# Threshold attention into a leaky MLP on one Trainium2 core: 128-partition loads with heads p and p+4 paired, MoE in groups of 128 tokens fed each step, weight loads gated by step

## Chip, core and metric

The kernel runs on one core of one Trainium2 (trn2) chip. The metric is device time in microseconds (us); lower is better. A "run" below is one timed execution. A run over 1.5% above the fastest of the same kernel in the same rounds counts as slow: one run of the kernel before (671.7 us) did and is left out of the ratios. A kernel has one profiled execution, so a stage read from a profile carries more noise than a time. Profiles of kernels that have the same program up to the 18th step show that step up to about 5 us apart. I therefore do not interpret stage differences under about 5 us.

The profile's engine names are PE (TensorE, matrix products), PEld (its weight loads), DVE (VectorE), ACT (ScalarE), POOL (GpSimd) and SP (SyncE, which issues most of the DMA transfers). L189 is a line of the kernel. A "chain of waits" is the work that ended last, followed back piece by piece to what released it.

## The reference

```python
# q, k, v: (8 batches, 8 heads, 576 rows, 64), float32; tau = 0.02
scores = q @ k^T / 8
scores = where(scores >= rowmax - tau, scores, -1e9)
attn   = softmax(scores);  x = (attn @ v), heads joined -> (4608 tokens, 512)
h = x @ w_in                     # w_in (512, 2048)
out = max(0.01*h, h) @ w_out     # w_out (2048, 512)
```

The kernel calls the second part the MoE, though it is one dense layer pair.

## The kernel before

Work proceeds in **steps**: one head pair times 128 query rows (the last 64 rows of two pairs share a step). There are 8 batches of 18 steps, 144 in all. A step does the scores (PE), a running max and shift (DVE), exp (ACT), a DMA transpose of the weights w into wt on SP's queue, and four steps later the product pv. In the profile's lines km and qm are the loaded k and q, sc the scores, sf and mx the scaled scores and their row maximum, P the shifted scores, xT the attention's result, hp and op the products of the hidden and output units below, gT the hidden values. k and q are split into high and low fp16 parts and transposed by DMA into kst and qst.

```python
def load_pair(src, store, nm, b, p):          # 64 partitions per load, heads 2p and 2p+1
    hb, g = divmod(p, 2)
    ...
    nc.sync.dma_start(out=store[b, hb][ds(64 * g, 64), :, :],
        in_=src[b, ds(2 * p, 2), :, :].rearrange("h (p t) d -> p h (t d)", t=9))
```

The MoE is cut into hidden units (h, 8 matmuls of 256 columns for a group of 256 tokens) and output units (o). The leak 0.01*h costs no vector work: `relu(0.99 h)` goes through w_out, and `x @ W_io`, with W_io = 0.01 * w_in @ w_out, is one more matmul in each output unit. W_io must be built first, from four DMA transposes of w_in (winT) and 64 matmuls (wiop).

```python
for g in range(4):                            # 1 MB each of float32, cast on the way
    at(1 + g // 2, lambda g=g: load_w_in(g))  # at(s, f): f is issued at the end of step s
    at(3 + g // 2, lambda g=g: load_w_out(g))
for g in range(2):
    at(6 + g, lambda g=g: wio_turn(g))
...
credit = min(credit + (1.1 if live else 2.0), 2.5)
if s >= 8 and wq:                             # W_io is built in steps 8 to 15
    hu = [wq.popleft(), wq.popleft()]
while credit >= 1.0 and (hq or oq):
    f = next_h(); ...
    f = next_o() if not wq and s >= 16 else None
```

Of the kernel before, what the change touches and what calls it, by code (L numbers as in the profile page):

```python
# [16 lines left out]
def kernel(  # L17
# [18 lines left out]

    nc = tc.nc
    B, H, S, D = q.shape
    tau_f = float(tau)
    NP = H // 2  # L40
# [3 lines left out]
    LAG = 4  # L44
    NJ = DF // 128
    NEG = -1025.0
    NW = 4

# [25 lines left out]
    def load_pair(src, store, nm, b, p):  # L74

        hb, g = divmod(p, 2)
        if (b, hb) not in store:
            store[b, hb] = sb.tile([128, 2, 576], FP32, tag=nm, bufs=2, name=nm)
        nc.sync.dma_start(  # L79
            out=store[b, hb][ds(64 * g, 64), :, :],  # L80
            in_=src[b, ds(2 * p, 2), :, :].rearrange("h (p t) d -> p h (t d)", t=9))

    def load_v(b, i):

        if i == 0:
            vts[b] = vbufs[b % 2]
        vt = vts[b]
        sv = v[b, :, :, :].rearrange("(g h) (p t) d -> h p g (t d)", h=2, t=9)
        out_, in_ = [
            (vt[0:64, :, 0, 0:5, :], sv[0][:, :, 0:320]),  # L90
            (vt[64:128, :, 0, 0:4, :], sv[0][:, :, 320:576]),
            (vt[64:128, :, 1, 0:5, :], sv[1][:, :, 0:320]),
            (vt[0:64, :, 1, 1:5, :], sv[1][:, :, 320:576]),
        ][i]
        nc.gpsimd.dma_start(out=out_, in_=in_)
# [53 lines left out]
    anchor = [None]  # L149

    def after_anchor(ins):

        if anchor[0] is not None:
            tc.add_manual_dep(
                ins.ins, anchor[0].ins.name,
                mybir.DependencyInfo(mybir.DependencyClass.Sync, mybir.DependencyReason.DATA), reason="port")


    class Group:
        def __init__(self, n, stores):  # L160
            self.n = n
            self.x = sb.tile([128, 4, n], FP16, tag=f"xT{n}", bufs=5 if n == 256 else 2, name="xT")
            self.g = None
            self.stores = stores
# [5 lines left out]
    def next_h():  # L170

        if hq and (hq[0][1] > 0 or live_g[0] < 2):
            f, u = hq.popleft()
            if u == 0:
                live_g[0] += 1
            return f
# [9 lines left out]
    late = []  # L186
    tail = [False]
# [3 lines left out]
    def h_unit(G, u):  # L191
        n = G.n
        per = 512 // n

        def mms():
            if u == 0:
                G.g = sb.tile([128, NJ, 256], FP16, tag="gT", bufs=2, name="gT")[:, :, 0:n]
            hp = ps.tile([128, per, n], FP32, tag="h", bufs=2, name="hp")
            for jj in range(per):
                j = u * per + jj  # L200
                for g in range(4):
                    mm(hp[:, jj, :], w_in16[:, g, ts(j, 128)], G.x[:, g, :], g == 0, g == 3)

            def act():
                nc.scalar.activation(out=G.g[:, ds(u * per, per), :], in_=hp, func=AF.Relu, bias=0.0, scale=0.99)  # L205
                if (u + 1) * per == NJ:
                    for m in range(n // 128):
                        for c in range(4):
                            oq.append((lambda m=m, c=c: o_unit(G, m, c), m == n // 128 - 1 and c == 3))
# [3 lines left out]
    def o_unit(G, m, c):  # L213
        if c == 0:
            if tail[0]:
                t = len(late) % 4
                late.append(0)
                G.op = ps.tile([128, 2, 512], FP32, tag=f"sc{t % 2}", bufs=1, name="op")[:, 0, :] if t < 3 else ps.tile([128, 512], FP32, tag="o", bufs=1, name="op")
            else:
                G.op = ps.tile([128, 512], FP32, tag="o", bufs=1, name="op")  # L220
        mm(G.op, G.x[:, c, ds(128 * m, 128)], w_io16[:, c, :], c == 0, False)
        for j in range(4 * c, 4 * c + 4):
            mm(G.op, G.g[:, j, ds(128 * m, 128)], w_out16[:, j, :], False, j == NJ - 1)
        if c == 3:
            op = G.op

            def fin():
# [5 lines left out]
                return lambda: nc.sync.dma_start(out=G.stores[m], in_=osb)  # L233
# [10 lines left out]
    def wio_unit(g, c):  # L244
        def mms():
            if c == 0:
                w_inT["ps", g] = ps.tile([128, 512], FP32, tag="o", bufs=1, name="wiop")
            p_ = w_inT["ps", g]
            for j in range(4 * c, 4 * c + 4):
                mm(p_, w_inT[g][:, j, :], w_out16[:, j, :], j == 0, j == NJ - 1)  # L250
            if c == 3:
                if g + 2 < 4:
                    wio_turn(g + 2)
                return lambda: nc.scalar.activation(out=w_io16[:, g, :], in_=p_, func=AF.Copy, bias=0.0, scale=0.01)
            return None
# [18 lines left out]
    def group_of(b, c):  # L274

        if c == 4:
            key = ("t", b // 4)
            if key not in groups:
                t = b // 4
                groups[key] = Group(256, [rows_of(4 * t + 2 * m, 4) for m in range(2)])  # L280
            return groups[key], 64 * (b % 4), b % 4 == 3
        if (b == B - 1 and c >= 2) or (b == 0 and c < 2):
            if (b, c) not in groups:
                groups[b, c] = Group(128, [rows_of(b, c)])
            return groups[b, c], 0, True
        key = (b, c // 2, 0)
        if key not in groups:
            groups[key] = Group(256, [rows_of(b, 2 * (c // 2) + cc) for cc in range(2)])
        return groups[key], 128 * (c % 2), c % 2 == 1
# [26 lines left out]
    def pv(s):  # L316
# [17 lines left out]
        def evac():  # L334


            if c < 4:
                x_ = G.x[:, :, ds(col, 128)].rearrange("f g (p i) -> f g i p", i=2)
# [3 lines left out]
            else:  # L342
                m, i = divmod(col // 64, 2)
                x_ = G.x[:, :, ds(128 * m, 128)].rearrange("f g (p i) -> f g i p", i=2)[:, :, i, :]
# [4 lines left out]
            if done:  # L349
                for u in range(NJ * G.n // 512):  # L350
# [35 lines left out]
    R = [ds(0, 64), ds(64, 64)]  # L386
    for p in range(NP):
        load_pair(k, kms, "km", 0, p)
        load_pair(q, qms, "qm", 0, p)
    def prep(p, nm, eng):  # L390
        hb, r = p // 2, R[p % 2]
        for h in range(2):
            if eng == "pool":
                x64(nm, 0, hb, h, r)
            for part in PARTS[nm]:
                lo(nm, 0, hb, h, part, r, eng)
        turn(nm, 0, p)

    for p in range(4):
        hb, r = p // 2, R[p % 2]  # L400
        hi("k", 0, hb, r)
        hi("q", 0, hb, r, "act" if p else "dve")
    for p, nm, eng in ((0, "q", "dve"), (0, "k", "dve"), (1, "k", "dve"), (1, "q", "dve"),
                       (2, "q", "dve"), (2, "k", "pool"), (3, "k", "pool")):
        prep(p, nm, eng)
    at(0, lambda: prep(3, "q", "dve"))

    for b in range(1, B):
        s0 = 18 * (b - 1)
        for hb in range(2):  # L410
            t0 = s0 + 9 * hb
            for i, p in enumerate((2 * hb, 2 * hb + 1)):
                at(t0 - 7 + 2 * i, lambda b=b, p=p: load_pair(k, kms, "km", b, p))
                at(t0 - 6 + 2 * i, lambda b=b, p=p: load_pair(q, qms, "qm", b, p))
# [17 lines left out]
    def load_w_in(g):  # L432
        nc.gpsimd.dma_start(out=w_in16[:, g, :], in_=moe_w_in[ts(g, 128), :])

    def load_w_out(g):
        nc.gpsimd.dma_start(
            out=w_out16[:, ds(4 * g, 4), :],
            in_=moe_w_out[ds(512 * g, 512), :].rearrange("(j p) d -> p j d", p=128))

    for i in range(4):  # L440
        at(0, lambda i=i: load_v(0, i))
    for g in range(4):
# [125 lines left out]
```

## Time and profile before

Before: 667.9 us median (663.6 to 672.0, 4 runs); the profiled span is 666.1 us. I cut the span where the 18th, the 36th and the last step start their shift (`P<-sf,mx` on DVE).

| stage | before, us |
|---|---|
| start: first batch, to the 18th step | 129.3 |
| second batch | 70.2 |
| later six batches | 417.2 |
| tail, after the last step's shift | 49.4 |

The view of busy time by stretch, for these stages of the kernel before. Columns are the stretch, its length, the busy us of each engine, the granted PE clock, the share of the 16 DMA engines (1.08 in the start: the packets' times there sum to more than the stretch, so they overlap) and GB/s.

```profile
core 0: us, PE busy (x) PEld busy (x) DVE busy (x) ACT busy (x) POOL busy (x), PEclk, DMA share, GB/s
0.00:129.30 129.30, 56.27 (x585) 32.92 (x587) 62.44 (x178) 57.40 (x116) 39.02 (x56) 0.97 1.08 169
129.30:199.50 70.20, 59.26 (x632) 34.97 (x633) 52.14 (x168) 52.79 (x115) 18.70 (x24) 0.93 1.04 182
199.50:616.70 417.20, 369.15 (x4007) 221.91 (x4007) 313.61 (x1003) 322.46 (x700) 92.67 (x121) 0.96 0.98 166
616.70:666.10 49.40, 43.74 (x367) 27.39 (x364) 5.70 (x13) 14.22 (x27) 0.00 (x0) 0.99 0.18 54
```

In the start PE works 56 of 129 us while the DMA share is 1.08, which points to DMA as the limit. In the later batches PE works 88% of the time. In the tail PE works 44 of 49 us.

The chain of waits of before, in order of time: start us, length, what the chain waited on.

```profile
32.35 15.42 DMA km<-in_k_dram
...
50.98 15.03 DMA wt<-w
66.31 15.14 DMA wt<-w
...
85.94 5.56 DMA winT<-win
91.54 3.48 PE wiop L189 x8
95.02 1.79 PE hp L189 x32
98.05 1.83 PE wiop L189 x8
102.02 1.83 PE wiop L189 x8
```

The line `hp x32` shows that 32 matmuls of 128 columns take 1.79 us, 56 ns each.

Groups of instructions of before with shapes kept apart (busy us, mean ns of one, then the idle time before them):

```profile
L189 PE MATMUL hp<-xT,win 128*128 128x256 f16 x1024 | 133.2, 277 | 0.0
L189 PE MATMUL hp<-xT,win 128*128 128x128 f16 x256 | 16.6, 219 | 0.0
L189 PE MATMUL wiop<-wout,winT 128*128 128x512 f16 x64 | 16.8, 410 | 7.1 <-DMA winT<-win 7.1
L339 DVE TENSOR_TENSOR xT<-pv,wt 128x512 f16<-128x512 f32 x32 | 23.3, 727 | 12.9 <-PE pv L327 12.9
```

Busy time divided by count gives 130 ns for a matmul of 256 columns and 65 ns for one of 128: no loss from halving the group. The mean ns of one (277 and 219) is longer because consecutive matmuls overlap in the trace.

### The profile page before, as it was taken

The numbers are of one execution on the slowest core, as the hardware profiler recorded it, in microseconds if no ns is written. First come the engines' busy times: TensorE is split into PE (matmuls) and PEld (weight loads), VectorE is DVE, ScalarE is ACT, GpSimd is POOL, SyncE is SP. The second block draws the span as 40 slices with busy tenths as digits, with TensorE's granted clock in tenths as the row PEclk, the third lists the DMA queues.
The fourth block names the chain that finished last, engine by engine and source line by source line (L and its number), as shares of the span: only waits on it lengthen the run. The fifth ranks groups of instructions, "written<-read, shape, count | busy, mean of one in ns | idle before, by whom it ended". The sixth has DMA issues, their size and how long they took to land.

```text
span 666.1 us, 14773 instructions
## 1 busy us (share of the span) xinstructions
PE 528.4 (79%) x5584; PEld 317.2 (48%) x5584; DVE 433.9 (65%) x1358; ACT 446.9 (67%) x955; POOL 150.4 (23%) x200
## 2 busy tenths in 40 slices
PE   0203359879796979699879989799979996999997
PEld 0101236546363646355445645465645563656564
DVE  5605337858786878578765858678756976888201
ACT  5115238759786888678785868689767886878421
POOL 3605112113331332024211422133202420000000
PEclk9999979989898989799998989999989998999999
DMA  9999999999999999979996999999998999557301
GB/s 183 136 154 166 182 186 159 189 168 165 186 206 153 164 177 194 178 151 181 198 180 123 191 180 184 162 167 191 202 165 173 178 170 148 105 107 124 85 32 47
DMA packets 298887, 106.35 MB, mean 160 GB/s; under 512 B 275264, under 2 KB 285504, under 8 KB 298816
## 3 DMA queue, kind: packets, MB, share of 16 engines
q1 hardware_dynamic: 287424, 96.50, 83.0%
q0 software_dynamic: 11392, 8.92, 10.9%
q8 instruction: 43, 0.70, 0.4%
q14 instruction: 28, 0.23, 0.1%
HBM read 36.70 MB, written 9.44 MB: 69 GB/s over the span
## 4 chain that ended last, share of the span: by engine, by line
PE 51%; DMA 22%; DVE 12%; ACT 9%; SPq 3%; issue 2%; POOL 0%; ACTq 0%
PE op L189 19%; PE hp L189 14%; DMA wt<-w 13%; PE sc L303 10%; DVE sf L363 8%; PE pv L327 5%; DMA qst<-qs 5%; ACT P L492 3%; DMA km<-in_k_dram 3%; ACT w L481 3%; PE wiop L189 2%; DVE P L477 2%; SPq L79 1%; ACT ks L125 1%; PE sc L309 1%
## 5 line engine op out<-in xcount | busy, mean ns | idle before, releaser
L363 DVE TENSOR_SCALAR_CACHE_REDUCE sf<-sc 128x576 f32<-128x576 f32 x288 | 206.5, 754 | 133.8 <-PE sc L303 122.8
L481 ACT ACTIVATE w<-P 128x576 f16<-128x576 f16 x288 | 193.6, 675 | 29.6 <-DVE P L477 16.9
L303 PE MATMUL sc<-kst,qst 64*128 64x288 f16 x1536 | 132.0, 302 | 75.2 <-DMA qst<-qs 45.3
L492 ACT ACTIVATE P<-sf,bb 128x576 f16<-128x576 f32 x144 | 111.4, 773 | 78.0 <-DVE bb L488 72.7
L189 PE MATMUL op<-wout,gT 128*128 128x512 f16 x576 | 157.2, 398 | 0.0
L189 PE MATMUL hp<-xT,win 128*128 128x256 f16 (+1 forms) x1280 | 149.8, 265 | 0.0
L205 ACT ACTIVATE gT<-hp 128x512 f16<-128x512 f32 x144 | 85.2, 593 | 75.4 <-PE hp L189 73.7
L189 PEld LDWEIGHTS <-win 128*128 128x128 f16 x1280 | 115.8, 99 | 39.2 <-issue 3.3
L303 PEld LDWEIGHTS <-qst 64*128 64x128 f16 x1536 | 71.1, 98 | 128.0 <-DMA qst<-qs 65.4
L327 PE MATMUL pv<-wt,v 128*64 128x128 f16 (+1 forms) x1600 | 71.2, 224 | 48.4 <-DMA wt<-w 45.7
L327 PEld LDWEIGHTS <-v 128*64 128x64 f16 x1600 | 51.1, 114 | 83.7 <-issue 80.2
L189 PEld LDWEIGHTS <-gT 128*128 128x128 f16 x576 | 58.4, 101 | 62.0 <-issue 12.0
L490 DVE TENSOR_SCALAR P<-sf,mx 128x576 f16<-128x576 f32 x144 | 73.8, 512 | 0.0
L477 DVE TENSOR_SCALAR P<-P 128x1152 int16<-128x1152 int16 x144 | 66.0, 459 | 11.0 <-ACT P L492 4.1
L137 POOL TENSOR_TENSOR ks<-km,ks 128x320 f16<-128x320 f32 (+1 forms) x64 | 47.2, 758 | 92.6 <-DVE P L477 61.3
L189 PE MATMUL op<-wio,xT 128*128 128x512 f16 x144 | 58.1, 404 | 3.0 <-ACT osb L232 3.0
L131 POOL TENSOR_SCALAR km<-km 128x576 f32<-128x576 f32 (+1 forms) x32 | 22.4, 702 | 159.9 <-ACT ks L125 106.1
L137 POOL TENSOR_TENSOR qs<-qm,qs 128x576 f16<-128x576 f32 x28 | 35.8, 1278 | 87.0 <-DVE P L477 55.6
L481 ACT ACTIVATION_READ_ACCUMULATOR w<-P 128x1 f32 x288 | 54.8, 190 | 0.0
L125 ACT ACTIVATE ks<-km 128x640 f16<-128x640 f32 (+3 forms) x36 | 22.4, 672 | 26.6 <-DMA km<-in_k_dram 26.6
L495 DVE RECIPROCAL rc<-sm 128x2 f32<-128x2 f32 x144 | 22.8, 158 | 25.2 <-ACT w L481 24.3
L496 DVE TENSOR_SCALAR w<-rc 128x128 f16<-128x128 f32 x144 | 32.8, 228 | 5.1
(29 smaller groups left out, 239.4 us busy)
## 6 DMA issues: line engine op xcount, KB each, us to landing
km<-in_k_dram SPq DMA_DIRECT2D x32, 288.0 KB, 4.7
qm<-in_q_dram SPq DMA_DIRECT2D x32, 288.0 KB, 5.1
out_dram<-osb SPq DMA_DIRECT2D x36, 256.0 KB, 4.0
v<-in_v_dram POOLq DMA_DIRECT2D x16, 160.0 KB, 5.7
wt<-w SPq DMA_TRANSPOSE x144, 4.4
v<-in_v_dram POOLq DMA_DIRECT2D x16, 128.0 KB, 5.8
win<-in_moe_w_in_dram POOLq DMA_DIRECT2D x4, 512.0 KB, 11.2
wout<-in_moe_w_out_dram POOLq DMA_DIRECT2D x4, 512.0 KB, 15.5
```

The source lines that it names most:

```text
L125: nc.scalar.activation(out=dst, in_=src, func=AF.Copy, bias=0.0, scale=64.0)
L137: return nc.gpsimd.tensor_tensor(out=dst[:, h], in0=src[:, h], in1=h_[:, h], op=AX.subtract)
L189: nc.tensor.matmul(out=out_, lhsT=lhsT, rhs=rhs, start=start, stop=stop, skip_group_check=True)
L205: nc.scalar.activation(out=G.g[:, ds(u * per, per), :], in_=hp, func=AF.Relu, bias=0.0, scale=0.99)
L303: nc.tensor.matmul(out=sc[h][:, half, 0:288], lhsT=qsts[b, p][r, qi, ds(128 * c, 128)], rhs=ksts[b, p][r, ki, ks_], start=(i == 0), stop=( ...
L327: nc.tensor.matmul(out=pvp[ds(64 * h, 64), p + u, :], lhsT=vt[:, p + u, h, j, :], rhs=wt[:, 4 * h + j, ds(64 * u, n)], start=(j == 0), sto ...
L363: nc.vector.tensor_scalar(out=halves(sf), in0=sc[:, :, 0:288], scalar1=C, scalar2=None, op0=AX.mult, op1=AX.max, accum_out=mx)
L477: anchor[0] = nc.vector.tensor_scalar(out=pi, in0=pi, scalar1=NEG, scalar2=None, op0=AX.max)
L481: nc.scalar.activation(out=e["W"][:, ds(576 * h, 576)], in_=e["P"][:, h, :], func=AF.Exp, bias=exp_bias, scale=1.0, accum_out=sm[:, h : h ...
L490: nc.vector.tensor_scalar(out=d["P"][:, 0, :], in0=sa, scalar1=ma, scalar2=tau_f, op0=AX.subtract, op1=AX.add)
L492: nc.scalar.activation(out=d["P"][:, 1, :], in_=sB, func=AF.Identity, bias=bb, scale=1.0)
L496: nc.vector.tensor_scalar(out=e["W"][:, 1152:1280].rearrange("p (h r) -> p h r", h=2), in0=rc.unsqueeze(2).to_broadcast([128, 2, 64]), sca ...
```

## The change

The intent has three parts. Heads p and p+4 become a pair, so that one load covers 128 partitions with one regular pattern. MoE groups shrink to 128 tokens, so that one hidden and one output unit per step keep pace with the steps. Weight loads come in smaller pieces, each of which waits for a DVE instruction of its step (`after_anchor`). With this the first eight groups no longer use W_io: DVE adds their leak (`leak`), so output can start at step 12, and W_io is built in steps 24 to 30.

```diff
-    def load_pair(src, store, nm, b, p):
...
+    def load_half(src, store, nm, b, hb):
+        m = store[b, hb] = sb.tile([128, 2, 576], FP32, tag=nm, bufs=2, name=nm)
+        nc.sync.dma_start(
+            out=m, in_=src[b, :, :, :].rearrange("(h f) (p t) d -> f p h (t d)", h=2, t=9)[
+                ds(2 * hb, 2)].rearrange("f p h x -> (f p) h x"))
...
+    L1_GROUPS = set(range(8, 36))
+    WIO = 20
...
+    def leak():
+        for gv, hp in leaky:
+            nc.vector.scalar_tensor_tensor(out=gv, in0=hp, scalar=0.01, in1=gv, op0=AX.mult, op1=AX.add)
...
-            hp = ps.tile([128, per, n], FP32, tag="h", bufs=2, name="hp")
+            hp = ps.tile([128, 4, 128], FP32, tag="h", bufs=2, name="hp")
...
-        mm(G.op, G.x[:, c, ds(128 * m, 128)], w_io16[:, c, :], c == 0, False)
+        if G.l1:
+            mm(G.op, G.x[:, c, :], w_io16[:, c, :], c == 0, False)
...
+    for g in range(8):
+        at(2 + g // 2, lambda g=g: load_w_in(g % 2, g // 2))    # each piece waits for its step
+        at(6 + g // 2, lambda g=g: load_w_out(g))
...
-        credit = min(credit + (1.1 if live else 2.0), 2.5)
+        credit = min(credit + 1.0 + 0.25 * (len(hq) + len(oq) > 8), 2.0)
-        if s >= 8 and wq:
-            hu = [wq.popleft(), wq.popleft()]
+        if s >= WIO + 3 and wq and s % 2 == 0:
+            hu = [wq.popleft()]
...
-            f = next_o() if not wq and s >= 16 else None
+            f = next_o()
```

The preparation of batch 0 (cut here) now handles each half in one go on 128 partitions, all before step 0.

More of the change, by code (lines that the diff above doesn't have):

```diff
@@ L47 @@
     NW = 4
+    NG = 3
     sb = ctx.enter_context(tc.tile_pool(name="sb", bufs=1))
@@ L72, with after_anchor @@
     qss, kss = {}, {}
-    def load_pair(src, store, nm, b, p):
-        hb, g = divmod(p, 2)
-        if (b, hb) not in store:
-            store[b, hb] = sb.tile([128, 2, 576], FP32, tag=nm, bufs=2, name=nm)
+    def load_half(src, store, nm, b, hb):
+        m = store[b, hb] = sb.tile([128, 2, 576], FP32, tag=nm, bufs=2, name=nm)
         nc.sync.dma_start(
-            out=store[b, hb][ds(64 * g, 64), :, :],
-            in_=src[b, ds(2 * p, 2), :, :].rearrange("h (p t) d -> p h (t d)", t=9))
+            out=m, in_=src[b, :, :, :].rearrange("(h f) (p t) d -> f p h (t d)", h=2, t=9)[
+                ds(2 * hb, 2)].rearrange("f p h x -> (f p) h x"))
+    anchor = [None]
+    def after_anchor(ins):
+        if anchor[0] is not None:
+            tc.add_manual_dep(
+                ins.ins, anchor[0].ins.name,
+                mybir.DependencyInfo(mybir.DependencyClass.Sync, mybir.DependencyReason.DATA), reason="port")
     def load_v(b, i):
@@ L87, in load_v @@
         vt = vts[b]
-        sv = v[b, :, :, :].rearrange("(g h) (p t) d -> h p g (t d)", h=2, t=9)
+        sv = v[b, :, :, :].rearrange("(h g) (p t) d -> h p g (t d)", h=2, t=9)
         out_, in_ = [
@@ L94, in load_v @@
         ][i]
-        nc.gpsimd.dma_start(out=out_, in_=in_)
+        after_anchor(nc.gpsimd.dma_start(out=out_, in_=in_))
     PARTS = {"k": [(0, 5, 0), (5, 4, 1)], "q": [(0, 9, None)]}
@@ L147, in turn, with __init__ @@
         (ksts if nm == "k" else qsts)[b, p] = t
-    anchor = [None]
-    def after_anchor(ins):
-        if anchor[0] is not None:
-            tc.add_manual_dep(
-                ins.ins, anchor[0].ins.name,
-                mybir.DependencyInfo(mybir.DependencyClass.Sync, mybir.DependencyReason.DATA), reason="port")
     class Group:
-        def __init__(self, n, stores):
-            self.n = n
-            self.x = sb.tile([128, 4, n], FP16, tag=f"xT{n}", bufs=5 if n == 256 else 2, name="xT")
+        def __init__(self, rows):
+            self.l1 = len(groups) in L1_GROUPS
+            self.x = sb.tile([128, 4, 128], FP16, tag="xT", bufs=5, name="xT")
             self.g = None
-            self.stores = stores
+            self.rows = rows
     hq = deque()
@@ L170, in next_h @@
     def next_h():
-        if hq and (hq[0][1] > 0 or live_g[0] < 2):
+        if hq and (hq[0][1] > 0 or live_g[0] < NG):
             f, u = hq.popleft()
@@ L186 @@
     late = []
+    leaky = []
+    def leak():
+        for gv, hp in leaky:
+            nc.vector.scalar_tensor_tensor(out=gv, in0=hp, scalar=0.01, in1=gv, op0=AX.mult, op1=AX.add)
+        leaky.clear()
     tail = [False]
@@ L191, in h_unit @@
     def h_unit(G, u):
-        n = G.n
-        per = 512 // n
         def mms():
             if u == 0:
-                G.g = sb.tile([128, NJ, 256], FP16, tag="gT", bufs=2, name="gT")[:, :, 0:n]
-            hp = ps.tile([128, per, n], FP32, tag="h", bufs=2, name="hp")
-            for jj in range(per):
-                j = u * per + jj
+                G.g = sb.tile([128, NJ, 128], FP16, tag="gT", bufs=NG, name="gT")
+            hp = ps.tile([128, 4, 128], FP32, tag="h", bufs=2, name="hp")
@@ L201, in mms @@
+            for jj in range(4):
                 for g in range(4):
-                    mm(hp[:, jj, :], w_in16[:, g, ts(j, 128)], G.x[:, g, :], g == 0, g == 3)
+                    mm(hp[:, jj, :], w_in16[:, g, ts(4 * u + jj, 128)], G.x[:, g, :], g == 0, g == 3)
             def act():
-                nc.scalar.activation(out=G.g[:, ds(u * per, per), :], in_=hp, func=AF.Relu, bias=0.0, scale=0.99)
-                if (u + 1) * per == NJ:
-                    for m in range(n // 128):
-                        for c in range(4):
-                            oq.append((lambda m=m, c=c: o_unit(G, m, c), m == n // 128 - 1 and c == 3))
+                gv = G.g[:, ds(4 * u, 4), :]
+                nc.scalar.activation(out=gv, in_=hp, func=AF.Relu, bias=0.0, scale=0.99)
+                if not G.l1:
+                    leaky.append((gv, hp))
+                if u == 3:
+                    for c in range(4):
+                        oq.append((lambda c=c: o_unit(G, c), c == 3))
@@ L210, in mms, with o_unit @@
             return act
         return mms
-    def o_unit(G, m, c):
+    def o_unit(G, c):
         if c == 0:
-            if tail[0]:
-                t = len(late) % 4
-                late.append(0)
-                G.op = ps.tile([128, 2, 512], FP32, tag=f"sc{t % 2}", bufs=1, name="op")[:, 0, :] if t < 3 else ps.tile([128, 512], FP32, tag="o", bufs=1, name="op")
+            n = len(late) % 3 if tail[0] else 2
+            late.append(0)
+            if n < 2:
+                G.op = ps.tile([128, 2, 512], FP32, tag=f"sc{n}", bufs=1, name="op")[:, 0, :]
@@ L219, in o_unit @@
             else:
                 G.op = ps.tile([128, 512], FP32, tag="o", bufs=1, name="op")
-        mm(G.op, G.x[:, c, ds(128 * m, 128)], w_io16[:, c, :], c == 0, False)
+        if G.l1:
+            mm(G.op, G.x[:, c, :], w_io16[:, c, :], c == 0, False)
         for j in range(4 * c, 4 * c + 4):
-            mm(G.op, G.g[:, j, ds(128 * m, 128)], w_out16[:, j, :], False, j == NJ - 1)
+            mm(G.op, G.g[:, j, :], w_out16[:, j, :], j == 0 and not G.l1, j == NJ - 1)
         if c == 3:
@@ L232, in fin @@
                     nc.scalar.activation(out=osb, in_=op, func=AF.Copy, bias=0.0, scale=1.0)
-                return lambda: nc.sync.dma_start(out=G.stores[m], in_=osb)
+                return lambda: nc.sync.dma_start(out=G.rows, in_=osb)
             return fin
@@ L242, in wio_turn, with wio_unit @@
         w_inT[g] = t
-    def wio_unit(g, c):
+    def wio_unit(g):
         def mms():
-            if c == 0:
-                w_inT["ps", g] = ps.tile([128, 512], FP32, tag="o", bufs=1, name="wiop")
-            p_ = w_inT["ps", g]
-            for j in range(4 * c, 4 * c + 4):
+            p_ = ps.tile([128, 512], FP32, tag="h", bufs=2, name="wiop")
+            for j in range(NJ):
                 mm(p_, w_inT[g][:, j, :], w_out16[:, j, :], j == 0, j == NJ - 1)
-            if c == 3:
-                if g + 2 < 4:
-                    wio_turn(g + 2)
-                return lambda: nc.scalar.activation(out=w_io16[:, g, :], in_=p_, func=AF.Copy, bias=0.0, scale=0.01)
-            return None
+            if g + 2 < 4:
+                wio_turn(g + 2)
+            return lambda: nc.scalar.activation(out=w_io16[:, g, :], in_=p_, func=AF.Copy, bias=0.0, scale=0.01)
         return mms
@@ L274, in group_of @@
     def group_of(b, c):
-        if c == 4:
-            key = ("t", b // 4)
-            if key not in groups:
-                t = b // 4
-                groups[key] = Group(256, [rows_of(4 * t + 2 * m, 4) for m in range(2)])
-            return groups[key], 64 * (b % 4), b % 4 == 3
-        if (b == B - 1 and c >= 2) or (b == 0 and c < 2):
-            if (b, c) not in groups:
-                groups[b, c] = Group(128, [rows_of(b, c)])
-            return groups[b, c], 0, True
-        key = (b, c // 2, 0)
+        key = (b, c) if c < 4 else ("t", b // 2)
         if key not in groups:
-            groups[key] = Group(256, [rows_of(b, 2 * (c // 2) + cc) for cc in range(2)])
-        return groups[key], 128 * (c % 2), c % 2 == 1
+            groups[key] = Group(rows_of(b - b % 2 if c == 4 else b, c))
+        return groups[key], (64 * (b % 2) if c == 4 else 0), c < 4 or b % 2 == 1
     st = [dict() for _ in range(NS)]
@@ L337, in evac @@
             if c < 4:
-                x_ = G.x[:, :, ds(col, 128)].rearrange("f g (p i) -> f g i p", i=2)
+                x_ = G.x.rearrange("f g (p i) -> f g i p", i=2)
                 nc.vector.tensor_tensor(
@@ L342, in evac @@
             else:
-                m, i = divmod(col // 64, 2)
-                x_ = G.x[:, :, ds(128 * m, 128)].rearrange("f g (p i) -> f g i p", i=2)[:, :, i, :]
+                x_ = G.x.rearrange("f g (p i) -> f g i p", i=2)[:, :, col // 64, :]
                 nc.vector.tensor_tensor(
@@ L349, in evac @@
             if done:
-                for u in range(NJ * G.n // 512):
+                for u in range(4):
                     hq.append((h_unit(G, u), u))
@@ L383, in at @@
         tick.setdefault(max(0, s), []).append(f)
-    R = [ds(0, 64), ds(64, 64)]
-    for p in range(NP):
-        load_pair(k, kms, "km", 0, p)
-        load_pair(q, qms, "qm", 0, p)
-    def prep(p, nm, eng):
-        hb, r = p // 2, R[p % 2]
-        for h in range(2):
-            if eng == "pool":
-                x64(nm, 0, hb, h, r)
-            for part in PARTS[nm]:
-                lo(nm, 0, hb, h, part, r, eng)
-        turn(nm, 0, p)
-    for p in range(4):
-        hb, r = p // 2, R[p % 2]
-        hi("k", 0, hb, r)
-        hi("q", 0, hb, r, "act" if p else "dve")
-    for p, nm, eng in ((0, "q", "dve"), (0, "k", "dve"), (1, "k", "dve"), (1, "q", "dve"),
-                       (2, "q", "dve"), (2, "k", "pool"), (3, "k", "pool")):
-        prep(p, nm, eng)
-    at(0, lambda: prep(3, "q", "dve"))
+    for hb in range(2):
+        load_half(k, kms, "km", 0, hb)
+        load_half(q, qms, "qm", 0, hb)
+    for hb in range(2):
+        hi("k", 0, hb)
+        hi("q", 0, hb, ALL, "dve" if hb == 0 else "act")
+        for nm in ("kq" if hb else "qk"):
+            for h in range(2):
+                for part in PARTS[nm]:
+                    lo(nm, 0, hb, h, part, ALL, "dve")
+        for g in range(2):
+            turn("q", 0, 2 * hb + g)
+            turn("k", 0, 2 * hb + g)
     for b in range(1, B):
@@ L411 @@
             t0 = s0 + 9 * hb
-            for i, p in enumerate((2 * hb, 2 * hb + 1)):
-                at(t0 - 7 + 2 * i, lambda b=b, p=p: load_pair(k, kms, "km", b, p))
-                at(t0 - 6 + 2 * i, lambda b=b, p=p: load_pair(q, qms, "qm", b, p))
+            at(t0 - 7, lambda b=b, hb=hb: load_half(k, kms, "km", b, hb))
+            at(t0 - 5, lambda b=b, hb=hb: load_half(q, qms, "qm", b, hb))
             t0 = s0 + 1 + 8 * hb
@@ L430, with load_w_in @@
             at(s0 + 6 + i, lambda b=b, i=i: load_v(b, i))
-    def load_w_in(g):
-        nc.gpsimd.dma_start(out=w_in16[:, g, :], in_=moe_w_in[ts(g, 128), :])
+    def load_w_in(h, c):
+        after_anchor(nc.gpsimd.dma_start(
+            out=w_in16[ds(64 * h, 64), :, ds(512 * c, 512)],
+            in_=moe_w_in[ds(256 * h, 256), ds(512 * c, 512)].rearrange("(g d) c -> d g c", d=64)))
     def load_w_out(g):
-        nc.gpsimd.dma_start(
-            out=w_out16[:, ds(4 * g, 4), :],
-            in_=moe_w_out[ds(512 * g, 512), :].rearrange("(j p) d -> p j d", p=128))
+        after_anchor(nc.gpsimd.dma_start(
+            out=w_out16[:, ds(2 * g, 2), :],
+            in_=moe_w_out[ds(256 * g, 256), :].rearrange("(j p) d -> p j d", p=128)))
     for i in range(4):
-        at(0, lambda i=i: load_v(0, i))
-    for g in range(4):
-        at(1 + g // 2, lambda g=g: load_w_in(g))
-        at(3 + g // 2, lambda g=g: load_w_out(g))
-    for g in range(2):
-        at(6 + g, lambda g=g: wio_turn(g))
-    wq = deque(wio_unit(g, c) for g in range(4) for c in range(4))
+        at(1, lambda i=i: load_v(0, i))
+    for g in range(8):
+        at(2 + g // 2, lambda g=g: load_w_in(g % 2, g // 2))
+        at(6 + g // 2, lambda g=g: load_w_out(g))
+    wq = deque()
+    if L1_GROUPS:
+        for g in range(2):
+            at(WIO + 2 * g, lambda g=g: wio_turn(g))
+        wq.extend(wio_unit(g) for g in range(4))
     credit = 0.0
@@ L455 @@
         stores = []
-        credit = min(credit + (1.1 if live else 2.0), 2.5)
+        credit = min(credit + 1.0 + 0.25 * (len(hq) + len(oq) > 8), 2.0)
         hu, ou, fins = [], [], []
-        if s >= 8 and wq:
-            hu = [wq.popleft(), wq.popleft()]
-        while credit >= 1.0 and (hq or oq):
+        if s >= WIO + 3 and wq and s % 2 == 0:
+            hu = [wq.popleft()]
+        while credit >= 1.0:
             f = next_h()
@@ L492 @@
             nc.scalar.activation(out=d["P"][:, 1, :], in_=sB, func=AF.Identity, bias=bb, scale=1.0)
+        leak()
         if 0 < s <= NS:
@@ L525 @@
         for nx in (next_o, next_h):
+            leak()
             f = nx()
```

## The prediction

> **What bounds it now.** A step is one head pair times 128 query rows; there are 144, in eight batches of 18. Three stages have different limits.
>
> - Start, 0 to about 130 us (18 steps). Busy time by stretch: PE works 27 of the first 100 us while the DMA share is 0.93 to 1.26. The chain of waits holds km loads (5.3, then 15.4 us), two W transposes of 15 us each and the first winT transpose (5.6 us): 8 MB of weights are queued from 26 us on, ahead of what the next step needs.
> - Middle, 130 to 617 us: about 70 us per batch. In the timeline an undisturbed full step takes 3.30 us with PE full (scores about 0.9, pv 0.5, one output unit about 1.1, one hidden unit about 1.0), so 18 steps need 59.4; the rest is waits for wt and qst transposes (4 to 6 us each in the chain) and steps with two units (5.3 us) or without one (2.8 us, DVE/ACT).
> - Tail, 617 to 666 us: only MoE. In instruction order 19 hidden and 24 output units are still due after the last scores: 19 x 0.97 + 24 x 1.09, about 45 us of PE.
>
> **What the change does.**
>
> 1. Groups of 128 tokens, one hidden and one output unit per step. Still 144 units of each; a hidden unit becomes 16 matmuls of 128 columns instead of 8 of 256. The 128-column form already runs in before: 32 in 1.79 us, so 0.9 us per unit, no loss. In instruction order 11 hidden and 15 output units remain after the last scores, about 27 us: the tail shrinks by about 18 us. The even feed removes double steps: 1 to 2 us per batch.
> 2. Weights gated by step (2 to 9), k/q of both halves loaded and prepared before step 0 on DVE. The same bytes move, but not ahead of the transposes; winT leaves the start. My sum of DMA work for the first 18 steps (W 27 us, wt 30, qst/kst 22, k/q 15, v 8, from packet times) is about 100 us. I expect the 18th step at about 104 us instead of 130: minus 26.
> 3. Loads over 128 partitions, 32 instead of 64. [...] Here k/q packets of 2304 B take 115 ns median, about 80 us of 16 engines in all; transposes take 437. So the gain is small: 1 to 2 us per batch.
> 4. No W_io for the first 8 groups: 32 matmuls fewer (7 us of PE), but 32 DVE leaks of about 0.73 us (like the 128x512 xT product). DVE needs about 2.95 us a step; with a leak and xT about 3.8, over PE's 3.1. About 16 of those steps are past the DMA-bound start. The wio matmuls (16 us) move from the DMA-bound start into steps 24 to 30, partly in place of missing units. Second batch: plus 8 us or more (78 to 80 instead of 70).
>
> **Sum.** 668 - 18 - 26 - 15 (six later batches) + 8 = about 616. Range 597 to 637; faster 0.94, within 2% 0.05, slower 0.01.
>
> **What would show it.** 18th step at 98 to 110 us; second batch longer than 70 us with DVE leading; later batches 66 to 69 us; after the last scores about 30 us, not 49; k/q packets shorter than 115 ns; hidden matmuls about 56 ns each.
>
> **What would make it wrong.** Gated weights landing late, so that PE waits for weights at steps 8 to 15; bigger loads delaying wt transposes past the four steps of lag; weight loads limiting the 128-column matmuls[...].

The 1 to 2 us per batch of point 3 are the author's estimate from the 80 us of packet time; that a load over 128 partitions is faster had not been shown when it was made.

## More of the kernel before

Preparation of the next batch's k and q is spread over the steps of the current one; the change leaves this part alone:

```python
t0 = s0 + 1 + 8 * hb                          # s0: first step of the current batch; hb: half
at(t0, hi k); at(t0 + 2, hi q)
# lo parts on POOL at t0+1 .. t0+8;  turn(k) at t0+5, t0+6;  turn(q) at t0+9, t0+10
```

## The result

After: 626.5 us median (624.2 to 628.3, 4 runs) against 667.9, ratio 0.938, 95% interval 0.931 to 0.945. All ratios here are the mean time of one kernel's fast runs over that of the other's of the same rounds, so not quite the ratio of the quoted medians.

| stage | before | after | difference | forecast |
|---|---|---|---|---|
| start | 129.3 | 103.8 | -25.5 | -26 |
| second batch | 70.2 | 79.7 | +9.5 | +8 |
| later six batches | 417.2 | 410.1 | -7.1 | -15 |
| tail | 49.4 | 32.9 | -16.5 | -18 |

Busy time by stretch of the kernel after, same stages and columns:

```profile
0.00:103.80 103.80, 50.23 (x560) 33.74 (x561) 60.78 (x182) 51.52 (x108) 33.32 (x52) 0.97 1.09 195
103.80:183.50 79.70, 70.15 (x828) 43.38 (x826) 60.20 (x185) 55.94 (x121) 18.55 (x24) 0.96 1.08 182
183.50:593.60 410.10, 374.35 (x4913) 248.01 (x4911) 319.54 (x1011) 325.09 (x706) 92.77 (x120) 0.95 0.99 170
593.60:626.50 32.90, 27.11 (x287) 17.87 (x284) 5.02 (x12) 9.28 (x17) 0.00 (x0) 0.99 0.22 55
```

PE works 27.1 us in the tail instead of 43.7. The six later batches are shorter although they carry 5 us more of PE work. In the second batch PE carries 11 us more, and the batch is 9.5 us longer.

Groups of after, shapes kept apart:

```profile
L201 PE MATMUL hp<-xT,win 128*128 128x128 f16 x2304 | 159.7, 225 | 0.0
L201 PE MATMUL wiop<-wout,winT 128*128 128x512 f16 x64 | 15.5, 398 | 0.0
L196 DVE SCALAR_TENSOR_TENSOR gT<-hp,gT 128x512 f16<-128x512 f32 x32 | 21.9, 684 | 0.0
```

The hidden matmuls cost 69 ns each (159.7 us over 2304), 160 us in all against 150 (133.2 + 16.6). That sum includes matmuls at half clock (57.1 us of the span have it); in the undisturbed steps of the tail (granted clock 0.99) a hidden unit takes about 0.9 us, start to start of its neighbours, as forecast.

The chain of waits of after, the longest pieces of the start and the W_io build of the second batch:

```profile
38.96 27.96 DMA wt<-w x2
67.90 9.31 DMA wt<-w
...
131.29 3.46 PE wiop L201 x16
134.75 5.96 DMA wt<-w
...
142.88 4.45 PE wiop L201 x16
...
152.57 3.56 PE wiop L201 x16
...
163.03 3.45 PE wiop L201 x16
```

The start still waits for two W transposes for 28 us, gate or no gate. The W_io build has left the start and lies on the chain of the second batch, 14.9 us in four pieces.

From the trace's packet records: the 2304-byte packets of k and q take 93 ns median and 125 mean, against 115 and 157 before. The DMA transposes, 266,240 packets of 256 B in both kernels, sum to about 440 us of 16 engines in both.

### The profile page after: what moved, and what is told of

The parts are those of the page before. It is cut to its first block, busy times and chain, and to the rows that moved or that the text cites. A ratio compares the mean times of both kernels' runs of the same rounds, so it can differ in the third digit from the quotient of the medians.

```text
span 626.5 us, 16727 instructions
## 1 busy us (share of the span) xinstructions
PE 521.8 (83%) x6576; PEld 343.0 (55%) x6576; DVE 445.5 (71%) x1385; ACT 441.8 (71%) x950; POOL 144.6 (23%) x196
## 3 DMA queue, kind: packets, MB, share of 16 engines
q1 hardware_dynamic: 286912, 96.50, 85.6%
## 4 chain that ended last, share of the span: by engine, by line
PE 46%; DMA 24%; DVE 16%; ACT 8%; SPq 4%; issue 2%; ACTq 0%; DVEq 0%
DMA wt<-w 17%; PE op L201 16%; PE hp L201 12%; PE sc L300 9%; DVE sf L359 8%; PE pv L324 5%; DMA qst<-qs 5%; SPq L156 3%; ACT w L473 3%; ACT P L484 2%; PE wiop L201 2%; DVE P L469 2%; DVE gT L196 2%; PE sc L306 1%; ACT qs L137 1%
## 5 line engine op out<-in xcount | busy, mean ns | idle before, releaser
L300 PE MATMUL sc<-kst,qst 64*128 64x288 f16 x1536 | 129.6, 304 | 52.8 <-DMA kst<-ks 23.0
L201 PEld LDWEIGHTS <-win 128*128 128x128 f16 x2304 | 147.9, 101 | 35.6 <-issue 4.4
L201 PE MATMUL hp<-xT,win 128*128 128x128 f16 x2304 | 159.7, 225 | 0.0
L201 PE MATMUL op<-wout,gT 128*128 128x512 f16 x576 | 155.1, 393 | 0.2 <-ACT osb L243 0.2
L201 PEld LDWEIGHTS <-gT 128*128 128x128 f16 x576 | 55.3, 100 | 55.0 <-issue 7.2
L149 POOL TENSOR_TENSOR ks<-km,ks 128x320 f16<-128x320 f32 (+1 forms) x56 | 39.8, 730 | 83.7 <-DVE P L469 55.8
L143 POOL TENSOR_SCALAR km<-km 128x576 f32<-128x576 f32 x28 | 18.7, 669 | 150.8 <-ACT ks L137 109.8
L201 PE MATMUL op<-wio,xT 128*128 128x512 f16 x112 | 44.8, 400 | 1.0 <-ACT osb L243 0.8
L489 DVE TENSOR_SCALAR w<-rc 128x128 f16<-128x128 f32 x144 | 32.6, 227 | 5.0
L143 POOL TENSOR_SCALAR qm<-qm 128x576 f32<-128x576 f32 x28 | 18.7, 669 | 65.4 <-DVE P L469 65.4
L336 DVE TENSOR_TENSOR xT<-pv,wt 128x512 f16<-128x512 f32 x32 | 23.3, 727 | 10.7 <-PE pv L324 10.7
## 6 DMA issues: line engine op xcount, KB each, us to landing
wout<-in_moe_w_out_dram POOLq DMA_DIRECT2D x8, 256.0 KB, 10.4
```

The lines of the kernel that those rows point to most:

```text
L143: return nc.gpsimd.tensor_scalar(out=m, in0=m, scalar1=64.0, scalar2=1.0, op0=AX.mult, op1=AX.mult)
L149: return nc.gpsimd.tensor_tensor(out=dst[:, h], in0=src[:, h], in1=h_[:, h], op=AX.subtract)
L201: nc.tensor.matmul(out=out_, lhsT=lhsT, rhs=rhs, start=start, stop=stop, skip_group_check=True)
L300: nc.tensor.matmul(out=sc[h][:, half, 0:288], lhsT=qsts[b, p][r, qi, ds(128 * c, 128)], rhs=ksts[b, p][r, ki, ks_], start=(i == 0), stop=( ...
L489: nc.vector.tensor_scalar(out=e["W"][:, 1152:1280].rearrange("p (h r) -> p h r", h=2), in0=rc.unsqueeze(2).to_broadcast([128, 2, 64]), sca ...
```

## Experiments

Twelve kernels ran, all correct, in three rounds each. A time is the median of four runs; the ratio is to the kernel before in the same rounds.

| kernel | time | ratio [95%] | 18th step | second batch | later six | tail |
|---|---|---|---|---|---|---|
| before | 667.9 | | 129.3 | 70.2 | 417.2 | 49.4 |
| after | 626.5 | 0.938 [0.931, 0.945] | 103.8 | 79.7 | 410.1 | 32.9 |
| halves | 635.0 | 0.954 [0.947, 0.962] | 112.1 | 79.9 | 407.6 | 32.8 |
| ungated | 626.2 | 0.941 [0.935, 0.947] | 104.9 | 80.0 | 408.6 | 32.8 |
| halves_ungated | 633.9 | 0.948 [0.943, 0.952] | 108.3 | 81.9 | 406.7 | 32.8 |
| before_wide | 659.1 | 0.986 [0.981, 0.991] | 126.7 | 67.7 | 413.2 | 49.4 |
| wio_early | 634.8 | 0.947 [0.942, 0.953] | 124.0 | 68.6 | 408.7 | 32.6 |
| wio_all | 630.5 | 0.943 [0.936, 0.949] | 120.2 | 70.3 | 405.0 | 33.2 |
| no_wio | 616.6 | 0.921 [0.912, 0.930] | 108.6 | 67.8 | 410.1 | 30.3 |
| late_o | 642.0 | 0.965 [0.958, 0.971] | 107.1 | 85.6 | 413.0 | 32.6 |
| late_o_flat | 642.9 | 0.961 [0.957, 0.965] | 107.6 | 79.6 | 409.6 | 44.1 |
| early_half | 612.1 | 0.920 [0.914, 0.927] | 103.7 | 80.6 | 391.8 | 32.5 |
| early_nowio | 608.8 | 0.910 [0.904, 0.917] | 105.1 | 68.0 | 402.5 | 30.3 |
| one_early_nowio | 604.6 | 0.904 [0.896, 0.912] | 104.5 | 69.0 | 400.2 | 30.6 |

### 1. What made the start shorter

**ungated**: the gate undone.

```diff
-        at(1, lambda i=i: load_v(0, i))
+        at(0, lambda i=i: load_v(0, i))
-    at(2 + g // 2, load_w_in) ; at(6 + g // 2, load_w_out)      # with after_anchor(...)
+    at(1 + g // 4, load_w_in) ; at(3 + g // 4, load_w_out)      # without
```

> The changed kernel, but v and the weights are queued as early as before (v at step 0, w_in at steps 1 and 2, w_out at steps 3 and 4) and without the wait for the step's DVE instruction. My theory (weights queued ahead of the transposes hold up the start): two W transposes again wait about 15 us each, the 18th step starts at 118 to 130 us instead of 103.7, nothing else moves, time 640 to 652. Rival (the k/q preparation of all halves before step 0 is the gain of the start): 18th step within 6 us of 103.7 and the time within 2% of 626.

Measured: 626.2 us and the 18th step at 104.9. My theory fell. The two longest waits of its chain sum to 28 us, as in after:

```profile
38.44 11.63 DMA wt<-w
50.85 16.80 DMA wt<-w
```

The ninth step does start later (71.6 us instead of 65.6), but by the 18th step the difference is gone. The weights' 26 us of packet time are the same in both kernels, and a queue that is full anyway (DMA share 1.10 up to the 18th step, 1.09 in after) does them sooner or later; the gate only reorders it. The rival named the early preparation of k and q. This run shows only that the gate is not the cause.

**halves**: each 128-partition load split in two.

```diff
-        nc.sync.dma_start(out=m, in_=<heads 2hb, 2hb+1 and their partners, 128 partitions>)
+        for f in range(2):
+            nc.sync.dma_start(out=m[ds(64 * f, 64), :, :], in_=src[b, ...][2 * hb + f])
```

> The changed kernel, but each k or q load of 128 partitions is issued as two loads of 64 partitions at the same step (layout, pairing and everything else as changed). My theory ([...] the start gained by the order of the weight loads): k/q packets of 2304 B go back from 93 ns median towards 115, the 18th step still starts within 6 us of 103.7, the later six batches grow by 0 to 8 us in sum, and the time is 626 to 640. Rival (the 128-partition loads are the main gain of the start and of the middle): 18th step at 115 us or later and the time 645 or more.

Measured: 635.0 us, inside my range, with the 18th step at 112.1, between the two theories. The packets rose past the old 115 ns to 148 ns median (their mean, 153 ns, is near the 157 of before). So the load shape is worth more in the start than I had it and nothing that shows in the later batches (407.6 against 410.1).

**before_wide**: this part alone in the kernel before (w_in has to come in halves of 64 partitions with it).

```diff
-    load_pair(k, kms, "km", 0, p) ...            # 64 partitions, heads 2p, 2p+1
+    load_half(k, kms, "km", 0, hb) ...           # 128 partitions, heads p, p+4
```

> The kernel before with one part of the change alone: heads paired as p and p+4, so that k and q are loaded over 128 partitions in 32 loads of twice the size (w_in therefore comes in halves of 64 partitions; preparation, MoE and weight order as before). Theory after the first four runs (the start is bound by DMA work, and the wide loads take about 10 us of packet time out of it): k/q packets fall from 115 to about 93 ns median, the 18th step from 129.3 to about 118 to 123, later batches by 0 to 1 us each, time 655 to 663. Rival (the loads matter only together with the new preparation order): 18th step within 4 us of 129 and the time within 1% of 667.

Measured: 659.1 us, ratio 0.986, inside the range. The 18th step came at 126.7, not the 118 to 123 that I expected, and the rest of the 9 us is spread over the other batches in amounts too small to place. The packets fell to 93 ns. By undoing (halves, 9 us) and by doing alone (9 us) the wide loads are worth about 9 us of the 41.

**halves_ungated**: both undone, to see whether gate and loads interact.

> The changed kernel with both parts undone: loads of 64 partitions, and the weights queued early without the wait. Theory (the gate only reorders a queue that is full anyway, so the two do not interact): 18th step at 110 to 116 us, the same as with halves alone (112.1), time 632 to 638. Rival (the gate guards against the slower loads): 18th step at 118 us or more, time 641 or more.

Measured: 633.9 us, 18th step at 108.3 (the forecast range began at 110; within profile noise). They do not interact.

**wio_early**: the ungated kernel, with W_io built in the start as before.

```diff
-    WIO = 20        # transposes at steps 20 and 22, matmuls at steps 24, 26, 28, 30
+    WIO = 5         # transposes at steps 6 and 7 (the next two follow), matmuls at steps 8, 10, 12, 14
```

> The changed kernel with weights queued early (as in the run without the gate, 626 us) and W_io built in the start as before: its transposes at steps 6 and 7 and its matmuls in steps 8, 10, 12 and 14. It tests what moving W_io out of the start gave and cost. Theory (W_io costs its four transposes of DMA and 14 us of PE wherever it stands, and only a part is hidden in the start): the 18th step goes from 104.9 to 114 to 122 us, the second batch from 80 to 64 to 70, the sum within 4 us of the run without the gate. Rival as forecast (in the start it was nearly free, and moving it cost 8 us): 18th step within 5 us of 104.9, second batch near 68, time 612 to 618.

Measured: the 18th step goes from 104.9 to 124.0, the second batch from 80.0 to 68.6, the time from 626.2 to 634.8. The rival, which is my forecast's reading, fell. My theory had the direction, but the sum is 8.6 us worse, not within 4: W_io costs 19 us in the start and 11 in the second batch. Its busy time by stretch, first two stages:

```profile
0.00:124.00 124.00, 60.98 (x623) 36.40 (x624) 61.30 (x181) 53.84 (x112) 33.47 (x52) 1.00 1.04 183
124.00:192.60 68.60, 55.19 (x763) 36.95 (x761) 60.17 (x185) 53.51 (x117) 18.67 (x25) 0.98 1.07 174
```

In the start PE has 61 us of work (47 without the build) in 124 us, so PE is not full. Yet the chain of waits of this kernel holds the four pieces and the wait for the first transpose:

```profile
72.52 7.34 DMA winT<-win
79.91 5.53 PE wiop L201 x16
...
90.00 3.56 PE wiop L201 x16
...
100.46 3.45 PE wiop L201 x16
...
110.12 3.45 PE wiop L201 x16
```

16 us of matmuls stand in the steps' PE order, ahead of the next scores. Here the average idle time of PE did not hide work that stands in front of the next link of the chain. The transposes also lengthen the DMA queue: four winT are 8192 packets of 256 B, and at the 18 ns median or the 27 ns mean they are an estimated 9 to 14 us of 16 engines. No run separates the matmuls from the transposes.

**wio_all**: no leaks; W_io serves all groups, so it must be built early, and output waits for it.

```diff
-    L1_GROUPS = set(range(8, 36)) ; WIO = 20 ; one unit every second step
+    L1_GROUPS = set(range(36))    ; WIO = 8  ; one unit per step
-            f = next_o()
+            f = next_o() if not wq else None
```

> The changed kernel with no leak at all: W_io serves all groups, built at steps 11 to 14, and output units start only then. If the leaks let W_io leave the start, and that is where the start gained, taking them away brings it back: 18th step at 116 to 126 us instead of 103.8, second batch 64 to 71 instead of 80, about three output units late: time 626 to 642. If leaks are a net cost, as the forecast's plus 8 us has it: 612 to 622.

Measured: 630.5 us, 18th step at 120.2, second batch 70.3: as expected. The leaks are what lets W_io leave the start; together they move 16 us out of the start and put 9 into the second batch.

### 2. What the longer second batch is

**no_wio**: no W_io, all 36 groups leak on DVE.

```diff
-    L1_GROUPS = set(range(8, 36))
+    L1_GROUPS = set()
```

> The changed kernel without W_io at all: every group takes the leak on DVE (144 leaks instead of 32), and the four transposes, the 64 wio matmuls and the 112 products of xT with W_io fall away. It measures the leak, which the forecast charged with the longer second batch. Forecast's reading (a leak step is bound by DVE at about 3.8 us): second batch still near 76 or more, later batches 70 or more each, time 640 to 660. Reading after the first eight runs (the 80 us of the second batch are the build of W_io; a leak step costs 3.3 us and 3.9 in every fourth): second batch 64 to 70, later six batches 0 to 4 us longer each, time 610 to 632.

Measured: 616.6 us, below the kernel after. The second batch is 67.8 us instead of 79.7, and the later six batches take 410.1 us in both kernels, with 100 more leaks in them. The stretches of no_wio:

```profile
108.60:176.40 67.80, 56.10 (x765) 37.78 (x763) 59.94 (x185) 53.57 (x116) 18.65 (x24) 0.97 1.04 182
176.40:586.40 410.00, 354.33 (x4822) 241.52 (x4820) 364.74 (x1111) 324.16 (x705) 93.63 (x120) 0.96 0.99 170
```

Over the later batches DVE has 45 us more work and PE 20 us less than in after, and the time is the same. Since PE had less to do, this does not show that a leak is free in itself; section 5 comes back to this. A leak step takes 3.3 us, and 3.9 in every fourth step (with the xT product). W_io's build is the whole of the longer batch.

The timeline of after shows how the forecast's 3.8 for each leak step went wrong. Consecutive DVE instructions overlap: a 0.75 us instruction at 130.09 is followed by the next at 130.76. From one step's first `sf` to the next (135.62 to 138.91), DVE takes 3.29 us without a pause, 0.62 of it for the xT product. A leak takes up 0.61 us before the next instruction starts:

```profile
132.05 0.69 DVE L196 SCALAR_TENSOR_TENSOR gT<-hp,gT 128x512 f16<-128x512 f32 x1
132.66 0.15 DVE L488 RECIPROCAL rc<-sm 128x2 f32<-128x2 f32 x1
```

From these figures I estimate 2.7 us of DVE for a plain step, 3.3 with a leak and 3.9 with a leak and xT, as the steps of no_wio show. So 3.8 was about right for a step with both, but only every fourth leak step has both; the others keep up with PE's 3.3.

### 3. Whether the tail is work

**late_o**: the nine output units of steps 12 to 20 held back.

```diff
-            f = next_o()
+            f = next_o() if s >= 21 else None
```

> The changed kernel, but output units may start only at step 21 instead of 12, so that nine output units are moved from the start, where PE has idle time, towards the end. My theory (the tail is the PE work still due after the last scores, and work taken in the start is free): the extra credit of the feed takes some of them back in the middle at 1.09 us each, the rest lies in the tail, so 5 to 12 us more: 631 to 639. Rival (the tail is latency of the last transposes and of the last group, not work): no change in the tail, 624 to 629.

Measured: 642.0 us, 15.5 us more, above my range, and the tail did not change. The extra credit of the feed gave the units back in the second and third batches (85.6 and 72.3 us, against 79.7 and 66.4), two per step. Read alone, this would fit the rival.

**late_o_flat**: the same without the extra credit.

```diff
-        credit = min(credit + 1.0 + 0.25 * (len(hq) + len(oq) > 8), 2.0)
+        credit = min(credit + 1.0, 2.0)
```

> As the run in which output units start at step 21 (642 us), but without the extra credit for a backlog, so that nothing is caught up in the middle. Theory (the tail is the PE work still due, not a latency): second and third batches return to 80 and 67 us or less, and the tail grows from 32.6 to about 42 us, nine units of 1.09 us; time 636 to 644. Rival (the tail is latency of the last group, with PE idle in it): tail 32 to 36 us and the time under 634.

Measured: 642.9 us; the tail is 44.1 us. The tail's stretch:

```profile
596.80:640.90 44.10, 37.48 (x369) 23.98 (x366) 5.69 (x13) 11.55 (x21) 0.00 (x0) 1.00 0.19 54
```

PE has 37.5 us of work in it instead of 27.1. The tail grew by 11.2 us with 10.4 us of PE work: the tail is the work still due, at about 1.2 us per unit. The work taken out earlier shortened nothing: the start has 543 matmuls instead of 560 and came at 107.6 us, the second batch 768 instead of 828 and took 79.6. The time rose by 16.4 us, 5 more than the tail; 4 of them stand in the start, within the noise of a profile, and their cause is open.

### 4. Why the later batches gained half of the forecast

In both kernels the third step of nearly every later batch takes 6 to 9 us and the fourth about 5. The timeline of after around such a step, SP's queue and PE:

```profile
257.58 1.61 SPq L156 DMA_TRANSPOSE qst<-qs  x1
259.37 2.18 SPq L373 DMA_TRANSPOSE wt<-w  x1
261.61 1.36 SPq L156 DMA_TRANSPOSE qst<-qs  x1
...
262.55 1.62 PE L300 MATMUL sc<-kst,qst 64*128 64x288 f16 x12 [3.79 <-DMA qst<-qs]
264.10 0.75 PE L324 MATMUL pv<-wt,v 128*64 128x64 f16 x20
264.78 0.61 PE L201 MATMUL op<-wio,xT 128*128 128x512 f16 x1
265.18 1.91 PE L201 MATMUL op<-wout,gT 128*128 128x512 f16 x4
```

The q transpose of pair 2 is issued at 257.6, one step ahead of the scores that need it; PE idles 3.8 us for it. After that the same score matmuls take 1.62 us instead of 0.91: the granted clock is 0.5 from 260.8 us on, for 6.83 us.

**early_half**: the second half of k and q is prepared two steps earlier, from the third batch on.

```diff
-            t0 = s0 + 1 + 8 * hb
+            t0 = s0 + 1 + (6 if b > 1 else 8) * hb
```

> The changed kernel, but from the third batch on the second half of the next batch's k and q is prepared two steps earlier. It tests why the middle gained 6.9 us and not the 15 forecast. Theory (a fixed lateness: the q transposes of pairs 2 and 3 are issued at the end of steps 0 and 1 of the batch that needs them at steps 2 and 3, which costs 4 to 8 us in each batch with the half clock after it, and neither kernel moves them): the third step of each later batch falls from 7 to 9 us to 3.5 or so, and 15 to 37 us go, time 590 to 612. Rival (DMA throughput bounds the middle, its share is near 1.0 there): the wait only moves to the wt transposes, and the time stays at 618 to 628.

Measured: 612.1 us, just outside my range of 590 to 612. In the six later batches the third step fell to between 3.3 and 3.9 us, and together they shrank from 410.1 to 391.8 us. The sum of the half-clock stretches in the trace, recorded from about 73 us on in after, fell from 57.1 to 24.9 us. How much of the gain is the clock and how much the wait itself was not measured apart. The waits of after, then those of early_half (us in total, times, longest):

```profile
PE pv L324 <- DMA wt<-w: 40.3, 21, 9.0
PEld L300 <- DMA qst<-qs: 35.6, 8, 12.9
PE sc L300 <- DMA qst<-qs: 21.4, 7, 3.9
```

```profile
PE pv L324 <- DMA wt<-w: 49.0, 24, 9.2
PEld L300 <- DMA qst<-qs: 15.8, 2, 12.9
PE sc L300 <- DMA qst<-qs: 2.7, 1, 2.7
```

The wait for qst is gone apart from the start and the second batch. A part moved to wt (40 to 49 us), so the rival has a share too: the DMA queue is nearly full (share 1.04 in these six batches, 0.99 in after), and some of what is no longer waited for in one place is waited for in another.

### 5. A version that beats both

**early_nowio** combines early_half with no_wio.

```diff
-    L1_GROUPS = set(range(8, 36))
+    L1_GROUPS = set()
-            t0 = s0 + 1 + 8 * hb
+            t0 = s0 + 1 + (6 if b > 1 else 8) * hb
```

> The second half of k and q prepared two steps earlier (the run of 612 us) and no W_io. If the two gains are separate (late q transposes in each batch; W_io's build in the second batch), they add: with a second batch of 64 to 70 us and the third steps of the later batches near 3.3, the time is 598 to 614. If DVE's leaks bind once the late transposes are gone, steps sit at 3.45 us or more and the time is 612 to 630.

Measured: 608.8 us. The gains add only in part (from 626.5, they are 14 and 10 us alone and 18 together): with a leak in each step the third steps are at 3.9, and three batches end with a step of about 9 us. The later six batches take 402.5 us here and 391.8 in early_half. About 7 of these 11 us lie in the batches' last steps, so how much a leak itself costs once the q transposes no longer stall stays open.

**one_early_nowio** uses one step instead of two, in every batch.

```diff
+            t0 = s0 + 1 + 7 * hb
```

> No W_io, and the second half of k and q prepared one step earlier instead of two, in every batch. The two-step version (609 us) still has steps of about 9 us at the end of three batches, where the k transposes and the next q load meet the W transposes in the queue. If one step is enough for the q transposes and spreads that traffic: third steps near 4 us, 18th steps of the batches below 6 us, time 598 to 607. If the wait is throughput and only moves about: 606 to 614.

Measured: 604.6 us, ratio 0.904. It is the best kernel here, 3.5% below the changed one. The third steps are at 3.9; the batches' last steps are between 3.3 and 7.5, not all below 6 as expected. Its interval overlaps that of the two-step version, so one step against two is not settled.

## Why the prediction was right or wrong

The time, 626.5 us, lies in the range of 597 to 637, 10 us above the point. Point by point:

- **Tail, "about 18 us": right, in size and mechanism.** Measured 16.5. The forecast had counted the units due after the last scores and multiplied by durations from the trace: about 27 us of PE. The profile shows 27.1, and late_o_flat shows that added work lengthens the tail one to one.
- **Start, "minus 26": right in size (25.5), wrong in cause.** The step that failed is "weights gated by step ... the same bytes move, but not ahead of the transposes". Taking the gate away changed nothing (ungated). The forecast named "winT leaves the start" in half a sentence; the W_io build is the largest part, 16 us (wio_all) to 19 (wio_early). The wide loads give a part that the profiles put at 3 to 8 us. What the new preparation order gives was not tested alone; with profile noise of 5 us, nothing that can be resolved is left for it. The nearest pair, before_wide and wio_early, have wide loads, early weights and W_io in the start alike, but not the preparation order (nor the MoE groups): they reach the ninth step at 80.8 and 73.1 us, the 18th at 126.7 and 124.0. What the new order gains early is within the noise by the 18th step. The agreement of the sum was luck: it was a sum of DMA work, and it left out that W_io's matmuls had stood on the chain.
- **Second batch, "plus 8": right in size (9.5), wrong in cause.** The step that failed is "with a leak and xT about 3.8, over PE's 3.1". Leak steps take 3.3, and 3.9 in every fourth, where the forecast charged 3.8 in each of 16. With leaks in all steps and no build the batch takes 67.8 us (no_wio), with leaks and the build 79.7. DVE does not lead in this batch, against the forecast's own sign: DVE is busy 60.2 of 79.7 us, PE 70.2. W_io's build, which the forecast let run "partly in place of missing units", is the whole price, so the agreement of the size was luck here too.
- **Later batches, "minus 15": wrong in size, measured minus 7, and most of the 10 us between point and time.** Two terms of 1 to 2 us per batch were expected. The loads gave nothing visible here (halves 407.6 against 410.1). The largest stall, the late q transpose with the half clock after it, is in a part of the schedule that the change does not touch. early_half took it away and gained 18 us in these batches. The forecast had listed "waits for wt and qst transposes" and then assumed, without checking when the transposes were issued, that lighter loads would ease them.
- **128-column matmuls cost nothing extra: right** where the clock is full (0.99 in the tail): a hidden unit takes about 0.9 us in the tail, 56 ns per matmul. "k/q packets shorter than 115 ns" was right too, 93.
- **Loads over 128 partitions, "1 to 2 us per batch": right in total** (about 9 us by before_wide and by halves), but it cannot be placed evenly over batches.

What the traces show of the transfers: a k or q packet of 2304 bytes took 93 ns median in the loads over 128 partitions (after, before_wide) and 115 to 148 ns in those over 64 (before, halves). The run halves issued two transfers for one and lost 9 us. The 256-byte transpose packets took 18 ns median and 26 to 27 ns mean, and a single W transpose in the start up to 20.1 us (before) or 18.1 us (after) from issue to landing, against 4.4 and 4.2 us median over the whole span.

What the trace of after shows of the clock: its half-clock stretches are 3.41, 6.83 or 10.24 us long, except where the span ends. Each of the ten before the end begins 2.1 to 3.6 us after PE went idle, for a wait such as the one for qst. Eight of these idle gaps of PE last 2.2 to 3.3 us, two 3.8 and 3.9; from 73 us on, where the clock is recorded, no other gap is over 2 us. That is no rule: in before one gap of 3.0 us (at 420.8) has no half clock with it.

## What to carry to other kernels

Here the DMA queue was full in the start (share 1.08 before, 1.09 after), and reordering it (the gate) gained nothing by the time it had drained; removing work from it, or from the chain's PE order, did (3 to 8 us of the start by the wide loads, 16 to 19 by the W_io build). Before you forecast that a lighter load will ease a recurring wait, look up when the awaited transfer is issued: the q transposes were issued one step of 3.3 us ahead of their use, took 4.6 us (median) to land, and came late with the lighter loads too. A precomputation that saves vector work has a price of its own, to be set against what the vector engine has to spare. Here dropping W_io, its build and its products with xT, gained 10 us, and 100 more leaks added nothing to the later batches; with the q transposes moved ahead it gained only 3 (612.1 to 608.8 us, and the intervals overlap).
